# One sink matmul per pair of heads in a fused attention and MLP kernel, and steady steps whose parts are ordered by eight lists

## The chip, the core and the metric

The kernel runs on one core of a Trainium2 chip. A core has a matrix engine (PE, with PEld for its weight loads), a vector engine (DVE), an activation engine (ACT), a general engine (POOL), a queue engine (SP) that issues most DMAs here, and two on-chip memories: SBUF, and PSUM with eight banks into which PE writes. Each engine runs its own instructions in program order and waits on semaphores for the others. The metric is the device time of one launch in microseconds (us); three runs of the kernel before took 714.06, 714.3 and 715.22 us, median 714.3.

## What is computed

Windowed attention with sink tokens (4 batches, 8 heads, 768 positions, head size 64), then a two-layer MLP with softplus on the joined heads:

```python
scores = scale * np.matmul(q, k.transpose(0, 1, 3, 2))
is_sink = pos[None, :] < int(n_sink)                 # n_sink = 4
in_window = (rel >= 0) & (rel < int(window))         # window = 128
scores = np.where(is_sink | in_window, scores, -1e9)
a = softmax(scores)                                  # with + 1e-9 in the denominator
x = (a @ v).transpose(0, 2, 1, 3).reshape(B * S, H * D)   # 3072 x 512
h = x @ w_in                                         # 512 -> 2048
g = np.maximum(h, 0.0) + np.log1p(np.exp(-np.abs(h)))
out = g @ w_out                                      # 2048 -> 512
```

## The kernel before

The 3072 rows are worked through in 12 chunks of 256 rows (three to a batch). A chunk has eight attention steps, one per head, and the MLP of a chunk runs one chunk later, also in eight steps, one per block of 256 of the 2048 hidden columns. So a steady step is one head of chunk k beside one block of chunk k - 1. The first two chunks are computed in plain fp32 ("exact" in the code); from the third chunk on every fp32 operand is split into a high part (fp32r) and a low part, and products are made of high and low parts: three matmuls for the MLP (`up` L495, `down_part` L546 to L548), two for the scores (L260, L261).

What a steady step does for head h of its chunk, with the letter that the code has for it:

- `p` (`split`) and `q` (`split_v`): high and low parts of the next heads' q, k and v (`qkh`, `kl`, `vv`).
- `S` (`scores`): four matmuls into two tiles `s`, four heads ahead. `T` (`softmax`): DVE masks the scores and takes the row minimum into `a` and `stats` (L275, L281), ACT takes the exponentials with their row sums (L282). `N` (`normalise`): DVE adds 1e-9 and takes reciprocals (`sm` L288, `rc` L289), mostly POOL scales `a` (L296).
- `W` (`weights_t`): PE transposes the weights of head h into the PSUM tile `t`; ACT copies the high part `th`, DVE takes the low part `tl`; POOL selects the band from both into `pt` (L340, L343).
- `k` and `K` (`sink_weights`, `sink`), once per four heads: DVE scales the weights of the eight sink columns (`sa` L301), PE transposes them into `ts`, ACT and DVE write high and low parts into rows 0 to 31 and 32 to 63 of the constant tile `sk`.
- `V` (`values`): PE accumulates into the PSUM tile `x`: first the sink matmul (L362, `sk` against the sink values `vs` of this one head), then three matmuls of `pt` against `vv` (L369).
- `O` (`out`): `x` holds three partial sums (rows 0 to 63 of its first and second half, rows 64 to 127 of its first half). ACT copies one of them to SBUF (`xt`), DVE adds the other two (L387, L388) into `xf`, which joins two heads. After an odd head ACT and POOL (DVE for the last head) take high and low parts `xh` and `xl`, the MLP's input.
- `U` (`up`): 24 matmuls into `h`. `F` (`softplus`): three ACT passes. `P` (`gate`): DVE makes `mt` (L510) and the high part `gh`; `R` (`residue`): DVE makes the low part `gl` a step later. `D` and `E` (`down`): six matmuls each into the two tiles `acc`, two steps behind `U`; after a chunk's last block both are copied and stored.

All eight PSUM banks are taken: two by `acc`, two by `h`, two by `s`, one by `t` and `ts` together, one by `x`. So the tiles `t` and `ts` follow each other in one bank, and so do the tiles `x` of successive heads.

Nothing reorders the work afterwards: each engine's program is in the order in which the code issues it. A list of letters written out by hand (`START`) gives it for the first part, up to step 16. From step 17 on (the 18th) a loop issues the loads of a step and then the letters of one of two lists, one for the first head of a chunk, the other for all the rest:

```python
Ctx.STEADY = ("kWRqpUKFSTDPNVOE", "kqWRpSDKTUFNPVEO")
for i in range(2 * H + 1, (n + 1) * H + lag + 1):
    for part in "JjGL" + c.STEADY[i % H == 0]:
        run, ahead = parts[part]
        run(i + ahead)
```

A letter issues everything that belongs to it, on all engines, at one place. Behind the letters of three of eight steps come two DVE reductions that check a split weight (`room`, L476).

Of the kernel before, what the change touches and what calls it, by code (L numbers as in the profile page):

```python
# [127 lines left out]
class _Attention:  # L128
# [10 lines left out]
    def load_sinks(self):  # L139
        c, nc, b = self.c, self.c.nc, self.b  # L140
        raw = c.lp.tile([64, 2, D], F32, tag="vsr", name=f"vsr{b}", bufs=1)
        nc.sync.dma_start(raw[:], c.a["vs"][b].unsqueeze(0).broadcast_to([2, 32, 2, D]))
        c.vsr[b] = raw

    def sinks(self, g):
# [11 lines left out]
        vs = c.vst[g] = c.lp.tile([P, G, P], F32R, tag=f"vs{g}", name=f"vs{g}", bufs=1)  # L157
        _zero(nc, vs[64:].rearrange("p (a e) d -> p a (e d)", a=2), c.sk[64:].bitcast(F32).unsqueeze(1).broadcast_to([64, 2, CT]))
        for part in range(2):
            self.sinks_place(g, part)  # L160

    def sinks_high(self):
        c, nc, b = self.c, self.c.nc, self.b
        c.vsh[b] = c.lp.tile([64, 2, D], F32R, tag="vsh", name=f"vsh{b}", bufs=1)
        nc.gpsimd.tensor_scalar(c.vsh[b][:], c.vsr[b][:], 1.0, 0.0, ALU.mult, ALU.add)
# [98 lines left out]
    def softmax(self, h):  # L264
# [11 lines left out]
        for j in range(CH):  # L276
# [5 lines left out]
            nc.scalar.activation(a, a, AF.Exp, bias=nm, scale=-1.0, accum_out=sm[:, j : j + 1])  # L282
# [41 lines left out]
    def weights_t(self, h):
# [3 lines left out]
        for j in range(CH):  # L328
            nc.tensor.transpose(t[:, j], self.a[h // G][:, h % G, j, :P], c.ident[:])  # L329
# [3 lines left out]
        if not self.exact:
            tl = c.sp.tile([P, CH, P], F32, tag="tl", name=f"tl{chunk}_{h}", bufs=1)
            _sub(nc, "V", tl[:], t[:], th[:])
            parts.append(tl)
# [11 lines left out]
    def values(self, h):  # L348
# [12 lines left out]
        if not (self.exact and odd):
            nc.tensor.matmul(x[:, 0], sv, self.sk[h // G], start=True, stop=False, skip_group_check=True)  # L362
        v = self.v[h // 2]
        for n in range(self.vlo, 3):
# [4 lines left out]
            nc.tensor.matmul(x[:, :, o], w, pt[:, :, m], start=False, stop=last, skip_group_check=True)  # L369
        self.x[h] = x  # L370

    def out(self, h):
# [14 lines left out]
        nc.vector.tensor_tensor(tmp[:], x[:D, 0], tmp[:], ALU.add)  # L387
        nc.vector.tensor_tensor(self.xf[r0 : r0 + D], x[:D, 1], tmp[:], ALU.add)  # L388
# [601 lines left out]
```

## Time and profile before

| what | value |
|---|---|
| median of three runs | 714.3 us |
| the profiled execution | 714.26 us, span 712.5 us |
| weights arriving and being split beside the first chunks, with gaps on PE | to about 107 us |
| attention beside the MLP | to about 656 us |
| the last MLP steps, without attention | to 705.5 us |

The largest group of each of three engines:

```profile
L495 PE MATMUL h<-xh,wi 128*128 128x256 f32 x1536 | 253.5, 287 | 0.4 <-DVE mt L510 0.4
L56 DVE TENSOR_TENSOR gl<-mt,gh 128x512 fp32r<-128x512 f32 x96 | 79.1, 824 | 0.2
L296 POOL TENSOR_SCALAR a<-a,rc 128x128 f32<-128x128 f32 x178 | 67.4, 391 | 184.0 <-DVE rc L289 156.4
```

These are rows of the groups of instructions: line, engine, operation, output and input by the names in the program with their shapes, count; then busy us in all and mean ns of one; then the idle time of the engine just before them and what ended it. A matmul's 287 ns runs to its modelled end, and the next one starts long before that, so the sum of such times is no time on the clock. POOL's 184 us of idle time ahead of its scaling cost nothing, since POOL waits there for work that comes once in a step.

### The profile page before, as it was taken

Reading aid. Unit: us, or ns where it says so; the run is one execution under the profiler, and the core shown is the slowest. Engines: PE = TensorE matmul, PEld = TensorE weight load, DVE = VectorE, ACT = ScalarE, POOL = GpSimd, SP = SyncE. Lnnn points to the kernel's source line nnn. Section 1 sums busy time; section 2 is a strip of 40 time slices with the busy share of each in tenths; the row PEclk is TensorE's granted clock in tenths of the full one; section 3 lists DMA queues with packets and bytes.
Section 4 is the critical chain, followed back from the end, with each engine's and each line's share of the span. In section 5 each row is a group of like instructions: output and inputs, shape, how many; then the busy total and the mean of one; then the engine's idle time right before and its main releaser. Section 6 shows DMA issues by size and latency. Waiting matters only on the chain.

```text
span 712.5 us, 13842 instructions
## 1 busy us (share of the span) xinstructions
PE 695.6 (98%) x4536; PEld 627.4 (88%) x4536; DVE 578.3 (81%) x1657; ACT 452.9 (64%) x1113; POOL 369.5 (52%) x676
## 2 busy tenths in 40 slices
PE   8998899999999999999999999999999999999996
PEld 7887779899989989899998989999998989999995
DVE  7999999888888987887887887888888888865541
ACT  5879866657666666666666666666666765753431
POOL 6767457555554555565555655564554555542000
PEclk9999999999999999999999999999999999999999
DMA  9985523213122221311321321312222221100001
GB/s 321 372 325 207 168 71 100 63 59 94 46 80 80 69 67 61 102 46 47 111 59 50 109 69 51 108 49 65 81 71 69 80 75 55 61 12 1 30 2 34
DMA packets 39341, 64.52 MB, mean 91 GB/s; under 512 B 4508, under 2 KB 19932, under 8 KB 39260
## 3 DMA queue, kind: packets, MB, share of 16 engines
q1 hardware_dynamic: 38826, 63.02, 28.0%
q8 instruction: 38, 0.62, 0.4%
q10 hardware_dynamic: 434, 0.52, 0.2%
q14 instruction: 43, 0.35, 0.2%
HBM read 57.24 MB, written 6.29 MB: 89 GB/s over the span
## 4 chain that ended last, share of the span: by engine, by line
PE 90%; DVE 4%; ACT 3%; DMA 1%; issue 0%; POOL 0%; SPq 0%; ACTq 0%; POOLq 0%
PE h L495 37%; PE acc L546 12%; PE acc L547 12%; PE acc L548 12%; PE x L369 5%; PE s L260 3%; PE s L261 3%; PE t L329 3%; PE x L362 2%; DMA wo50r<-w 1%; ACT a L282 1%; PE word_ps L660 1%; PE ts L313 1%; ACT upper L48 1%; PE s L257 1%; DVE wt L439 1%
## 5 line engine op out<-in xcount | busy, mean ns | idle before, releaser
L495 PE MATMUL h<-xh,wi 128*128 128x256 f32 x1536 | 253.5, 287 | 0.4 <-DVE mt L510 0.4
L495 PEld LDWEIGHTS h<-xh,wi 128*128 128x128 f32 x1536 | 211.2, 191 | 1.7 <-DVE mt L510 0.6
L296 POOL TENSOR_SCALAR a<-a,rc 128x128 f32<-128x128 f32 x178 | 67.4, 391 | 184.0 <-DVE rc L289 156.4
L495 PE MATMUL h<-xl,wi 128*128 128x256 f32 x768 | 154.8, 283 | 1.6 <-DVE xl L56 1.6
L546 PE MATMUL acc<-wo,gh 128*128 128x512 f32 x384 | 152.3, 397 | 0.3 <-ACT gh L48 0.3
L548 PE MATMUL acc<-wo,gl 128*128 128x512 f32 x384 | 150.8, 393 | 0.3 <-DVE gl L56 0.3
L547 PE MATMUL acc<-wo,gh 128*128 128x512 f32 x384 | 151.0, 393 | 0.0
L495 PEld LDWEIGHTS h<-xl,wi 128*128 128x128 f32 x768 | 119.5, 192 | 2.0 <-DVE xl L56 2.0
L502 ACT ACTIVATE mt<-h 128x512 f32<-128x512 f32 x96 | 57.0, 594 | 98.7 <-PE h L495 98.7
L510 DVE SCALAR_TENSOR_TENSOR mt<-h,mt 128x512 f32<-128x512 f32 x96 | 66.1, 689 | 63.8 <-ACT mt L504 56.1
L282 ACT ACTIVATE a<-a,stats 128x136 f32<-128x136 f32 x192 | 76.1, 397 | 38.9 <-DVE stats L281 38.9
L548 PEld LDWEIGHTS acc<-wo,gl 128*128 128x128 f32 x384 | 72.1, 188 | 17.9 <-DVE gl L56 1.2
L546 PEld LDWEIGHTS acc<-wo,gh 128*128 128x128 f32 x384 | 72.1, 188 | 13.5 <-ACT gh L48 0.8
L547 PEld LDWEIGHTS acc<-wo,gh 128*128 128x128 f32 x384 | 72.3, 188 | 8.8
L56 DVE TENSOR_TENSOR gl<-mt,gh 128x512 fp32r<-128x512 f32 x96 | 79.1, 824 | 0.2
L340 POOL TENSOR_SCALAR_AFFINE_SELECT pt<-tl 128x256 fp32r<-128x256 f32 x80 | 59.1, 738 | 23.0 <-DVE tl L56 22.7
L340 POOL TENSOR_SCALAR_AFFINE_SELECT pt<-th 128x256 fp32r<-128x256 f32 (+1 forms) x96 | 46.4, 483 | 40.4 <-ACT th L48 38.8
L503 ACT ACTIVATE mt<-mt 128x512 f32<-128x512 f32 x96 | 60.8, 633 | 3.1
L504 ACT ACTIVATE mt<-mt 128x512 f32<-128x512 f32 x96 | 60.7, 633 | 3.0
L48 ACT CAST qkh<-qk 128x656 fp32r<-128x656 f32 x80 | 59.5, 744 | 0.4 <-DMA qk<-qk 0.4
L56 DVE TENSOR_TENSOR kl<-qk,qkh 128x400 fp32r<-128x400 f32 x80 | 51.5, 644 | 2.5
L56 DVE TENSOR_TENSOR tl<-t,th 128x256 f32<-128x256 f32 x80 | 33.2, 414 | 23.3 <-ACT th L48 23.3
(191 smaller groups left out, 1248.3 us busy)
## 6 DMA issues: line engine op xcount, KB each, us to landing
qk<-qk SPq DMA_DIRECT2D x160, 164.0 KB, 3.0
out<-o SPq DMA_DIRECT2D x23, 256.0 KB, 2.2
vr<-v SPq DMA_DIRECT2D x28, 192.0 KB, 2.5
q<-q SPq DMA_DIRECT2D x7, 256.0 KB, 5.6
k<-k SPq DMA_DIRECT2D x8, 200.0 KB, 8.1
vz<-v SPq DMA_DIRECT2D x4, 384.0 KB, 7.9
vr<-v SPq DMA_DIRECT2D x12, 128.0 KB, 2.1
vz<-v SPq DMA_DIRECT2D x4, 256.0 KB, 4.1
```

The costliest lines, as they stand in the source:

```text
L48: nc.scalar.copy(out, in_)
L56: (nc.vector if eng == "V" else nc.gpsimd).tensor_tensor(out, a, b, ALU.subtract)
L282: nc.scalar.activation(a, a, AF.Exp, bias=nm, scale=-1.0, accum_out=sm[:, j : j + 1])
L296: (nc.vector if eng == "V" else nc.gpsimd).tensor_scalar(a, a, rc[:, j : j + 1], 0.0, ALU.mult, ALU.add)
L340: nc.gpsimd.affine_select(pt[:, e, :, 1], src[:], [[0, CH], [1, P]], ALU.is_ge, 0.0, base=0, channel_multiplier=-1)
L495: nc.tensor.matmul(h[:, j], wt, x, start=k == 0, stop=k >= len(prods) - 2, skip_group_check=True)
L503: nc.scalar.activation(t[:], t[:], AF.Exp, scale=-1.0)
L504: nc.scalar.activation(t[:], t[:], AF.Ln, bias=1.0)
L510: nc.vector.scalar_tensor_tensor(t[:], h[:], 0.0, t[:], ALU.max, ALU.add)
L546: nc.tensor.matmul(acc[:], gh[:, j, q], wh, start=f == 0, stop=False, skip_group_check=True)
L547: nc.tensor.matmul(acc[:], gh[:, j, q], wl, start=False, stop=False, skip_group_check=True)
L548: nc.tensor.matmul(acc[:], gl[:, j, q], wh, start=False, stop=f == 2 * FP - 1, skip_group_check=True)
```

## The change

Four things are changed together.

1. The sinks. The sink values `vs` keep one column block of 64 per head, and `vs` and `sk` use all 128 rows: rows 0 to 63 of `sk` are high and low parts as before, rows 64 to 127 a copy of them by POOL; the high part of the sink values stands behind rows 0 to 63, the low part behind 64 to 127. One matmul against the columns of two heads then gives the sink sums of a pair. It is issued for even heads only, into a tile `xs` in the bank of `t`, and ACT copies it into `xf`.
2. The sum. `x` no longer starts with the sink matmul. DVE adds the three parts of `x` to `xf` one after the other, and ACT's copy `xt` goes.
3. Steps in one-engine parts. A letter issues its first part, and the rest is kept under a small letter and issued where that letter stands: `h` (`ql`, `kl`), `Q` (`vl`), `e` (exponentials), `n` (scaling), `t` (`th`), `u` (`tl`), `B` (selects), `X` and `x` (`xh`, `xl`), `g` (`gh`), `Y` (stores).
4. Eight lists, one for each step of a chunk, in place of two. The list up to step 16 is the same.

```diff
+    def do(self, kind, step):
+        if self.later is None:
+            step()
+        else:
+            self.later.setdefault(kind, []).append(step)
+    def now(self, kind):
+        for step in self.later.pop(kind, ()):
+            step()
...
         if not self.exact:
             _sub(nc, "V", sk[G * NS : 2 * G * NS], t[: G * NS], sk[: G * NS])
+            _copy(nc, "P", sk[2 * G * NS :], sk[: 2 * G * NS])
...
             x = c.ps_x.tile([P, 2, CT], F32, tag="x", name=f"x{chunk}_{h}")[:]
-            sv = c.vs[self.b, h // G][:, h % G]
-        if not (self.exact and odd):
-            nc.tensor.matmul(x[:, 0], sv, self.sk[h // G], start=True, stop=False, skip_group_check=True)
+            if not odd:
+                sv = c.vs[self.b, h // G][:, h % G : h % G + 2].rearrange("p h d -> p (h d)")
+                t = c.ps_t.tile([P, CT], F32, tag="t", name=f"xs{chunk}_{h}")
+                nc.tensor.matmul(t[:], sv, self.sk[h // G], start=True, stop=True)
+                self.xs(h, t)
...
-        tmp = c.sp.tile([D, CT], F32, tag="xt", name=f"xt{chunk}_{h}", bufs=1)
-        _copy(nc, "A", tmp[:], x[D:, 0])
-        nc.vector.tensor_tensor(tmp[:], x[:D, 0], tmp[:], ALU.add)
-        nc.vector.tensor_tensor(self.xf[r0 : r0 + D], x[:D, 1], tmp[:], ALU.add)
+        xf = self.xf[r0 : r0 + D]
+        for part in (x[:D, 0], x[:D, 1], x[D:, 0]):
+            nc.vector.tensor_tensor(xf, part, xf, ALU.add)
...
+    def xs(self, h, t):
+        self.xf = c.sp.tile([P, CT], F32, tag="xf", name=f"xf{chunk}_{h}")
+        _copy(nc, "A", self.xf[:], t[:])
...
-            for part in "JjGL" + c.STEADY[i % H == 0]:
-                run, ahead = parts[part]
-                run(i + ahead)
+            for part in "JjGL" + c.STEADY[i % H]:
+                if part in parts:
+                    run, ahead = parts[part]
+                    run(i + ahead)
+                else:
+                    c.now(part)
...
-Ctx.STEADY = ("kWRqpUKFSTDPNVOE", "kqWRpSDKTUFNPVEO")
+Ctx.STEADY = [
+    "kWtuDpQSqTBKyhenURXNVFPEYOgx",
+    "WqtkQyuUSpDhTFEPKnRBgxVeXNYO",
...
```

What this does on the engines, at three places of chunk 7. A name such as `x7_2_5762` is the tile `x` of chunk 7, head 2, with a running number. First PE, where the values of head 2 begin, behind the first six down matmuls; before:

```order
L546 MATMUL acc6_1_5748<-wo00_512,gh6_0_5558 128x512
L547 MATMUL acc6_1_5748<-wo00_512,gh6_0_5558 128x512
L548 MATMUL acc6_1_5748<-wo00_512,gl6_0_5593 128x512
L362 MATMUL x7_2_5762<-sk_66,vs0_1342 128x256
L369 MATMUL x7_2_5762<-pt7_2_5693,vv7_1_5595 128x2x128
L369 MATMUL x7_2_5762<-pt7_2_5693,vv7_1_5595 128x512
```

and after the change, at the same place:

```order
L604 MATMUL acc6_1_5730<-wo00_516,gh6_0_5562 128x512
L605 MATMUL acc6_1_5730<-wo00_516,gh6_0_5562 128x512
L606 MATMUL acc6_1_5730<-wo00_516,gl6_0_5637 128x512
L405 MATMUL xs7_2_5741<-sk_66,vs0_1346 128x256
L414 MATMUL x7_2_5740<-pt7_2_5713,vv7_1_5570 128x2x128
L414 MATMUL x7_2_5740<-pt7_2_5713,vv7_1_5570 128x512
```

The sink matmul has kept its place for this even head and writes `xs`; at head 3 no such row is left ahead of the values.

Second DVE, from the making of `mt` for block 2 of chunk 6 to the low part `tl` of the next head; before:

```order
L510 SCALAR_TENSOR_TENSOR mt6_2_5730<-h6_2_5705,mt6_2_5730 128x512
L50 CAST gh6_2_5756<-mt6_2_5730 128x512
L288 TENSOR_SCALAR sm7_6_5740<-sm7_6_5740 128x2
L289 RECIPROCAL rc7_1_5516<-sm7_6_5740 128x2
L387 TENSOR_TENSOR xt7_2_5768<-x7_2_5762,xt7_2_5768 64x256
L388 TENSOR_TENSOR xf7_2_5767<-x7_2_5762,xt7_2_5768 64x256
L476 TENSOR_REDUCE room_64<-wi41_858 128x1 x2
L56 TENSOR_TENSOR tl7_3_5788<-t7_3_5783,th7_3_5786 128x256
L56 TENSOR_TENSOR gl6_2_5795<-mt6_2_5730,gh6_2_5756 128x512
```

and after the change:

```order
L563 SCALAR_TENSOR_TENSOR mt6_2_5718<-h6_2_5675,mt6_2_5718 128x512
L307 TENSOR_SCALAR sm7_6_5722<-sm7_6_5722 128x2
L308 RECIPROCAL rc7_1_5487<-sm7_6_5722 128x2
L59 CAST gh6_2_5750<-mt6_2_5718 128x512
L430 TENSOR_TENSOR xf7_2_5743<-x7_2_5740,xf7_2_5743 64x256 x3
L529 TENSOR_REDUCE room_64<-wi41_862 128x1 x2
L65 TENSOR_TENSOR gl6_2_5798<-mt6_2_5718,gh6_2_5750 128x512
L65 TENSOR_TENSOR tl7_3_5805<-t7_3_5770,th7_3_5803 128x256
```

Two adds have become three, and `gl` now stands ahead of `tl`.

Third DVE at the change of chunks, from `mt` of the last block of chunk 5 to the low part that goes into `sk` for heads 0 to 3 of chunk 7; before:

```order
L510 SCALAR_TENSOR_TENSOR mt5_7_5426<-h5_7_5401,mt5_7_5426 128x512
L50 CAST gh5_7_5450<-mt5_7_5426 128x512
L288 TENSOR_SCALAR sm7_3_5436<-sm7_3_5436 128x2
L289 RECIPROCAL rc7_0_5146<-sm7_3_5436 128x2
L387 TENSOR_TENSOR xt6_7_5460<-x6_7_5456,xt6_7_5460 64x256
L388 TENSOR_TENSOR xf6_6_5363<-x6_7_5456,xt6_7_5460 64x256
L56 TENSOR_TENSOR xl6_4778<-xf6_6_5363,xh6_4777 128x256
L301 TENSOR_TENSOR sa7_0_5477<-a7_0_5145,rc7_0_5146 128x64
L56 TENSOR_TENSOR tl7_0_5484<-t7_0_5479,th7_0_5482 128x256
```

and after the change:

```order
L563 SCALAR_TENSOR_TENSOR mt5_7_5404<-h5_7_5373,mt5_7_5404 128x512
L430 TENSOR_TENSOR xf6_6_5344<-x6_7_5436,xf6_6_5344 64x256 x3
L59 CAST gh5_7_5443<-mt5_7_5404 128x512
L307 TENSOR_SCALAR sm7_3_5420<-sm7_3_5420 128x2
L308 RECIPROCAL rc7_0_5128<-sm7_3_5420 128x2
L65 TENSOR_TENSOR xl6_4767<-xf6_6_5344,xh6_4766 128x256
L325 TENSOR_TENSOR sa7_0_5463<-a7_0_5127,rc7_0_5128 128x64
L65 TENSOR_TENSOR tl7_0_5470<-t7_0_5465,th7_0_5468 128x256
```

The adds now stand directly behind `mt`, and `gh`, `sm` and `rc` between the adds and `xl`.

More of the change, by code (lines that the diff above doesn't have):

```diff
@@ L90, in _constants @@
     make_identity(nc, c.ident)
-    c.hmask = cp.tile([64, G], F32, name="hmask")
+    c.hmask = cp.tile([P, G], F32, name="hmask")
     nc.gpsimd.memset(c.hmask[:], 1.0)
-    for e in (0, 32):
+    for e in range(0, P, 32):
         m = c.hmask[e : e + 32]
@@ L156, in sinks, with sinks_place @@
             self.sinks_low()
[L157 to L160, printed above, removed]
+        c.vst[g] = c.lp.tile([P, G, D], F32R, tag=f"vs{g}", name=f"vs{g}", bufs=1)
+        self.sinks_place(g)
     def sinks_high(self):
         c, nc, b = self.c, self.c.nc, self.b
-        c.vsh[b] = c.lp.tile([64, 2, D], F32R, tag="vsh", name=f"vsh{b}", bufs=1)
+        c.vsh[b] = c.lp.tile([P, 2, D], F32R, tag="vsh", name=f"vsh{b}", bufs=1)
         nc.gpsimd.tensor_scalar(c.vsh[b][:], c.vsr[b][:], 1.0, 0.0, ALU.mult, ALU.add)
     def sinks_low(self):
-        raw = self.c.vsr[self.b]
-        self.c.nc.gpsimd.tensor_tensor(raw[:], raw[:], self.c.vsh[self.b][:], ALU.subtract)
-    def sinks_place(self, g, part):
+        c, b = self.c, self.b
+        low = c.vsh[b][D:]
+        c.nc.gpsimd.tensor_tensor(low, c.vsr[b][D:], low, ALU.subtract)
+    def sinks_place(self, g):
         c, b = self.c, self.b
         c.vs[b, g] = c.vst[g]
-        src = (c.vsh, c.vsr)[part][b]
-        self._place(c.vst[g][:64, :, part * D : part * D + D], src[:, g : g + 1], 64)
+        self._place(c.vst[g][:], c.vsh[b][:, g : g + 1], P)
     def _place(self, out, src, rows):
@@ L281, in softmax, with exps @@
             nc.vector.tensor_tensor_reduce(a, self.s.pop((h, j))[:, :KW], m[:], -SCALE, BIG, ALU.add, ALU.min, nm)
-            nc.scalar.activation(a, a, AF.Exp, bias=nm, scale=-1.0, accum_out=sm[:, j : j + 1])
+        c.do("e", lambda: self.exps(h))
+    def exps(self, h):
+        c, nc = self.c, self.c.nc
+        for j in range(CH):
+            a = self.a[h // G][:, h % G, j]
+            k = (self.chunk * H + h) * CH + j
+            sm = self.sm[h][:, j : j + 1]
+            nc.scalar.activation(a, a, AF.Exp, bias=c.stats[:, k : k + 1], scale=-1.0, accum_out=sm)
     def normalise(self, h):
@@ L332, in weights_t, with weights_low, select @@
         parts = [th]
[L333 to L336, printed above, removed]
+        if self.exact:
+            c.do("B", lambda: self.select(h, parts))
+        else:
+            c.do("u", lambda: self.weights_low(h, t, parts))
+    def weights_low(self, h, t, parts):
+        c, nc, chunk = self.c, self.c.nc, self.chunk
+        tl = c.sp.tile([P, CH, P], F32, tag="tl", name=f"tl{chunk}_{h}", bufs=1)
+        _sub(nc, "V", tl[:], t[:], parts[0][:])
+        parts.append(tl)
+        c.do("B", lambda: self.select(h, parts))
+    def select(self, h, parts):
+        c, nc, chunk = self.c, self.c.nc, self.chunk
+        th = parts[0]
         lo = 1 if self.first else 0
@@ L368, in values @@
             last = n == 2 and (odd or not self.exact)
-            nc.tensor.matmul(x[:, :, o], w, pt[:, :, m], start=False, stop=last, skip_group_check=True)
+            first = n == self.vlo and not self.exact
+            nc.tensor.matmul(x[:, :, o], w, pt[:, :, m], start=first, stop=last, skip_group_check=True)
         self.x[h] = x
@@ L530, in down @@
                 if j == 1:
-                    self.store(t)
+                    self.store(t, self.acc[t])
             return
@@ L647, in next_sinks @@
             return
-        if k < n and att[k].first and 0 < e < 6:
+        if k < n and att[k].first and 0 < e < 5:
             a = att[k]
-            if e < 4:
-                (a.load_sinks, a.sinks_high, a.sinks_low)[e - 1]()
-            else:
-                a.sinks_place(0, e - 4)
-        elif att[k - 1].first and k - 1 > c.EXACT and e < 2:
-            att[k - 1].sinks_place(1, e)
+            (a.load_sinks, a.sinks_high, a.sinks_low, lambda: a.sinks_place(0))[e - 1]()
+        elif att[k - 1].first and k - 1 > c.EXACT and e == 0:
+            att[k - 1].sinks_place(1)
     def fill(n):
@@ L900, in _kernel @@
                 _fast(c)
-            c.last = False
+            c.last, c.later = False, None
         ok = nc.values_load(c.flag[:1, :1], min_val=0, max_val=1)
```

53 lines of the change are left out of this document (41 added, 12 removed).

## The prediction

> **What bounds the kernel now.** I read the page first: busy shares, the slices, the chain that ended last.
>
> ```profile
> span 712.5 us, 13842 instructions
> PE 695.6 (98%) x4536; PEld 627.4 (88%) x4536; DVE 578.3 (81%) x1657; ACT 452.9 (64%) x1113; POOL 369.5 (52%) x676
> PE   8998899999999999999999999999999999999996
> DVE  7999999888888987887887887888888888865541
> PEclk9999999999999999999999999999999999999999
> PE 90%; DVE 4%; ACT 3%; DMA 1%; issue 0%; POOL 0%; SPq 0%; ACTq 0%; POOLq 0%
> ```
>
> PE carries 90% of the chain, and its granted clock never falls, so the clock explains nothing here. A busy PE may still hide waits, so next come the busy times by stretch, PE's waits, and the chain in order of time inside the steady part.
>
> ```profile
> 50.00:100.00 50.00, 45.44 (x281) 39.04 (x280) 48.64 (x122) 42.69 (x97) 29.16 (x40) 1.00 0.54 173
> 158.38:325.32 166.94, 166.94 (x1110) 151.75 (x1110) 141.41 (x413) 110.09 (x273) 92.74 (x171) 1.00 0.24 72
> PEld ts L313 <- DVE tl L56: 0.7, 3, 0.2
> ...
> 246.44 2.88 PE h L495 x24
> ...
> 251.20 0.12 PE x L362
> 251.32 0.47 PE x L369 x3
> ...
> 253.18 0.22 PE t L329 x2
> ```
>
> The columns of the stretches are length, then PE, PEld, DVE, ACT and POOL busy. Before about 107 us PE has gaps. From there to 700 us it has none: the three chunks from 158.38 to 325.32 are full to the last digit, and the only wait recorded for PE between 107 and 700 us is that of the weight load of `ts`, 0.7 us in three cases. One step (one head, one block of the MLP) is 253.18 - 246.22 = 6.96 us of back-to-back matmuls. So in this stage a matmul taken off PE is worth its slot on the chain, as long as what feeds PE still comes in time. DVE is the next engine: 141.41 of 166.94 us, 85%.
>
> **The sink matmuls.** 80 of them (10 chunks of 8 heads) become 40.
>
> ```profile
> L362 PE MATMUL x<-sk,vs x80: 279/279/283, 105.1 to 652.9; 128*128 128x256 f32 x80
> ```
>
> The 279 ns is one matmul from start to modelled end; the next begins long before. What counts is its slot on the chain, 0.12 us above (251.20 to 251.32). 40 x 0.12 = **4.8 us** less. They run from 105.1 to 652.9 us, all but the first inside the full stretch, so nothing else hides them. Were each worth its whole 279 ns, the gain would be 11.2 us; the full stretch excludes that, since the spacing is seen.
>
> The Trainium skill ("TensorE: Matmul & The Clock Gate", Back-to-back issue gap) gives N/2.4 + 2.5 ns, 109 ns for N = 256, against 120 ns in the trace; by it the gain would be an estimated 4.4 us. The measured slot decides.
>
> **The adds.** Each head had one ACT copy (64x256) and two DVE adds; now it has three DVE adds, and each pair one ACT copy of 128x256.
>
> ```profile
> L48 ACT COPY xt<-x 64x256 f32<-64x256 f32 x80 | 29.7, 372 | 2.0
> L48 ACT CAST th<-t 128x256 fp32r<-128x256 f32 x79 | 29.6, 374 | 25.0 <-PE t L329 23.0 <-issue 1.1
> 232.04 0.40 DVE L387 TENSOR_TENSOR xt<-x,xt 64x256 f32<-64x256 f32 x1
> 232.47 0.42 DVE L388 TENSOR_TENSOR xf<-x,xt 64x256 f32<-64x256 f32 x1
> 232.81 1.26 DVE L476 TENSOR_REDUCE room<-wi 128x1 f32<-128x512 f32 x2
> ...
> 238.96 0.42 DVE L388 TENSOR_TENSOR xf<-x,xt 64x256 f32<-64x256 f32 x1
> 239.41 0.23 DVE L301 TENSOR_TENSOR sa<-a,rc 128x64 f32<-128x64 f32 x1
> ```
>
> ACT: 80 x 0.372 goes, 40 x 0.374 (the nearest copy of that shape) comes: 14.8 us less, off the path. DVE: a dependent add takes 0.43 us from start to start (232.04 to 232.47), so 80 x 0.43 = 34 us more. That costs nothing as long as it fits into DVE's idle time beside PE's matmuls. Over the three chunks DVE would be busy 141.4 + 24 x 0.43 = 151.7 us. PE then needs 166.94 - 12 x 0.12 = 165.5 us. DVE may thus idle 13.8 us, where it idled 25.5. Nearly half of its waits must go, or DVE becomes the bound. That is the main risk, and the lists decide it.
>
> After an add into the upper rows (odd heads) the next instruction starts 0.45 us on, after one into the lower rows 0.34 us on (the two pairs of rows above). The Trainium skill ("VectorE: DVE Perf Modes", Two Vector instructions with no wait between them) has a rule for this: an instruction whose input or output starts in another quadrant than the last one is held until all earlier ones end. The trace agrees. By that rule the third add, which reads `x` from row 64, holds its follower also in even heads: an estimated 0.1 us more for 40 heads, 4 us of DVE in all, 1.2 us of the 13.8. It speaks against the change but takes no sign from it.
>
> **The order.** Most lists keep PE's order (transposes, up, scores, down, values, down). What is moved is when DVE, ACT and POOL do their parts. On SP the order is unchanged, and the loads still open each step, so no transfer is moved. I look at three places.
>
> First `ts` in the step of head 0, the tightest of before:
>
> ```profile
> 265.20 0.69 DVE L510 SCALAR_TENSOR_TENSOR mt<-h,mt 128x512 f32<-128x512 f32 x1 [0.54 <-ACT mt L504]
> 266.97 0.42 DVE L388 TENSOR_TENSOR xf<-x,xt 64x256 f32<-64x256 f32 x1
> 267.86 0.43 DVE L56 TENSOR_TENSOR xl<-xf,xh 128x256 fp32r<-128x256 f32 x1 [0.47 <-ACT xh L48]
> 268.34 0.42 DVE L56 TENSOR_TENSOR tl<-t,th 128x256 f32<-128x256 f32 x1
> 267.42 0.41 ACT L48 CAST xh<-xf 128x256 fp32r<-128x256 f32 x1 [1.08 <-DVE xf L388]
> 268.98 0.38 PE L313 MATMUL ts<-ident,sa 128*32 128x128 f32 x2
> ```
>
> The bank of `t` is free at 268.34 + 0.42 = 268.76 us, and `ts` starts at 268.98. After the change the adds come right behind `mt`: 265.20 + 0.72, then 0.43 + 0.43 + 0.42 gives xf at 267.20; `xh` ends at 267.63. `gh`, `sm` and `rc` fill that wait (0.34 + 0.28), `xl` starts near 267.74, 0.12 earlier, and `tl` ends near 268.64. PE arrives 0.12 us earlier too, having one sink matmul less. The margin stays as it was: some 0.2 us, no stall but no room. The third add is paid by `mt`'s wait of 0.54 us and by the idle time at `xl`.
>
> Second, the bank of `t` now also takes the sink sums `xs` of even heads; the next head's transposes wait for ACT's copy of it.
>
> ```profile
> 249.36 0.60 ACT L502 ACTIVATE mt<-h 128x512 f32<-128x512 f32 x1 [1.40 <-PE h L495]
> 252.09 0.37 ACT L48 COPY xt<-x 64x256 f32<-64x256 f32 x1
> ```
>
> The up matmuls end at 249.32, and ACT is through softplus and exponentials at 252.09, 2.77 us on; the copy ends 3.14 us on. PE reaches the transposes at 253.18, 3.86 us on, so 0.7 us is to spare. In head 6 `xh` stands ahead of the copy (0.41 us): 0.3 us. In head 4 `sk` stands ahead of softplus, but `ts` delays PE as well: about 0.5 us. In head 0 the copy stands ahead of softplus and has over a microsecond.
>
> Third, `sk` gets a POOL copy (64x256) ahead of the sink matmul, 20 times.
>
> ```profile
> L165 POOL TENSOR_SCALAR vsh<-vsr 64x128 fp32r<-64x128 f32 x4 | 1.3, 318 | 5.4 <-DMA vsr<-vs 5.4
> L60 POOL TENSOR_SCALAR sk<-room 128x256 fp32r<-128x256 f32 x1 | 0.4, 397 | 0.0
> PE h L495 <- DVE xl L56: 1.6, 2, 1.1
> PE x L369 <- POOL pt L343: 0.4, 1, 0.4
> ```
>
> No row shows that copy; between 0.32 and 0.40 us I take 0.40, same free size. From head 0 on, up (2.88 us) lies between `ts` and `xs`, and from head 4 on, scores and down (1.9 us); ACT's and DVE's parts of `sk` plus 0.40 are about 1.7 us. It is hidden, by least in head 4.
>
> Chunk 2's first head still runs in the hand-ordered start. There `xs` follows `sk` closely and may wait 0.1 us (at most 0.4). The larger `hmask` adds four selects of about 0.19 us on POOL near the beginning, ahead of a wait of 2.0 us for the sink values' DMA, which covers them. POOL makes the sink weights with fewer operations, which could end PE's 0.4 us wait for `pt`; the 1.1 us wait for `xl` hangs on DVE. Bounds for the start: -0.4 to +1.2 us. I take +0.1.
>
> **Sum.** The profiled execution took 714.26 us, its span 712.5; the median of the three shown is 714.3, the same. 714.26 - 4.8 + 0.1 + 0.4 = 709.96, **710.0 us**. The 0.4 is my allowance for small stalls at the tight places: two more hand-overs of 0.23 us (0.7/3, the wait at `ts`).
>
> **Rivals.**
> Late hand-overs eat the gain. A chunk has four `xs` and two `ts`, 60 in all. If a third come late by 0.23 us, 20 x 0.23 = 4.6 us go: 714.1. For it: margins of 0.2 to 0.3 us. Against: a stall gives DVE and ACT time to catch up.
>
> DVE becomes the bound, and it gets slower. Price per three chunks:
>
> ```profile
> DVE mt L510 <- ACT mt L504: 10.1, 16, 1.4
> DVE tl L56 <- ACT th L48: 7.0, 9, 0.9
> DVE sm L288 <- ACT a L282: 2.2, 3, 0.7
> ```
>
> If only the 7.0 us at `tl` go and the other 18.5 of the 25.5 us stay, three chunks take 151.7 + 18.5 = 170.2 us, 3.3 more than now, and ten take 11 more: **725 us**. The point from which this decides: over 15.2 us of idle time left (166.94 - 151.7) is slower than before. For it: 0.43 us a head on an engine 85% busy, and the steps with two reductions (1.19 us from 232.81 to the next) fill DVE wholly. Against: the lists move `tl` behind `gl` or `sa` and the adds ahead of `gh`, so those waits are filled, as worked out at `ts`; odd steps have about 1 us to give back.
>
> The matmul's slot is not worth its time, PE being held by something that the records hide: 714.3 us. The unbroken chain speaks against it.
>
> **Chances.** Forecast 0.66 (709.1 to 712.8, up to 0.3 us of stalls a chunk), late hand-overs 0.14, DVE bound 0.17, hidden slot 0.03. A measurement of this kernel tells about 0.2% (1.4 us) from no change. Faster is the forecast, 0.66; same the second and the fourth, 0.17; slower 0.17. The range leaves out the DVE case and little else: from 708.9 (a little below 714.26 - 4.8 - 0.4 = 709.06) to 715.5 (the late hand-overs with the start's +1.2).
>
> **What would show it.** Right: the three-chunk stretch PE-full and about 1.4 us shorter, DVE near 92% busy, `tl`'s and `mt`'s waits below 14 us together. Wrong: waits of PE's weight loads at `t` on ACT's `xs` copy or at `ts` on DVE's `tl` (late hand-overs), or PE below 99% between 160 and 600 us behind `x`, `s` or `acc` with DVE as releaser (DVE bound). If PE is full and the steps are no shorter, the slot of the sink matmul was hidden.

## The result, and the profile after

The changed kernel is **slower** by 0.6%, clear of the noise: median 718.79 us (four runs, 718.53 to 719.29) against 714.23 us (four runs of before), ratio 1.0061, 95% interval 1.0046 to 1.0077. The forecast was 710.0 us. The page of the kernel after, its profiled execution 718.53 us, by the same rows as before:

```profile
span 716.7 us, 13788 instructions
...
PE 694.9 (97%) x4496; PEld 622.5 (87%) x4496; DVE 607.7 (85%) x1737; ACT 429.7 (60%) x1073; POOL 356.5 (50%) x690
...
PE   8998999999999999999999999999999999999996
...
DVE  7999989898998988988998998988998899876442
...
PE 71%; DVE 16%; ACT 3%; issue 2%; POOL 0%; DVEq 0%; POOLq 0%; ACTq 0%
```

PE still looks full in tenths, but its share of the chain fell from 90% to 71% and DVE's rose from 4% to 16%. The groups of after show the exchange itself:

```profile
L430 DVE TENSOR_TENSOR xf<-x,xf 64x256 f32<-64x256 f32 x240 | 100.6, 419 | 6.7
L405 PE MATMUL xs<-sk,vs 128*128 128x256 f32 x40 | 12.4, 310 | 0.7 <-POOL sk L61 0.7
L61 POOL TENSOR_SCALAR sk<-sk 64x256 fp32r<-64x256 f32 x20 | 9.2, 459 | 7.0 <-DVE sk L65 5.8 <-DVE s L286 0.6
```

40 sink matmuls, 240 adds, 20 copies of `sk`, as the diff says. Next the stretch of three chunks, from one `ts` of head 0 to the third after it, 166.94 us before (columns as there: length, then PE, PEld, DVE, ACT and POOL busy):

```profile
158.54:327.13 168.59, 166.82 (x1096) 150.51 (x1096) 150.25 (x437) 103.03 (x261) 88.88 (x176) 1.00 0.24 71
```

It is 1.65 us longer, not 1.4 shorter, and PE is no longer busy to its end. Which waits these are, from the waits of after between 110 and 655 us (before had there 0.7 us at `ts`, in three cases):

```profile
PEld ts L337 <- DVE tl L65: 7.3, 12, 1.0
PE ts L337 <- DVE tl L65: 4.7, 9, 0.7
PEld xs L405 <- POOL sk L61: 3.7, 10, 0.6
```

Nine waits of PE for `tl`, one in each chunk, at the one place that the prediction called the tightest: `ts` in the step of head 0. (The three more of the weight load are at `ts` of head 4.) The recorded idle time is not all of it, since a matmul's busy time runs to its modelled end: the last matmul of `s` in the rows below starts at 270.19, so `ts` could have followed 0.12 us later, at 270.31. It starts at 271.00, 0.69 us late where 0.53 are recorded. With 0.16 us more for each of nine, the 4.7 us are about 6.1. First PE, then DVE in the timeline of after, ahead of that `ts`:

```profile
270.19 0.28 PE L272 MATMUL s<-kl,qkh 128*128 128x264 f32 x1
271.00 0.39 PE L337 MATMUL ts<-ident,sa 128*32 128x128 f32 x2 [0.53 <-DVE tl L65]
```

```profile
257.98 0.55 DVE L286 COPY_PREDICATED s<-diag,s 128x128 f32<-128x128 int32 x2 [0.63 <-PE s L272]
...
259.93 0.68 DVE L563 SCALAR_TENSOR_TENSOR mt<-h,mt 128x512 f32<-128x512 f32 x1
...
260.99 0.70 DVE L307 TENSOR_SCALAR sm<-sm 128x2 f32<-128x2 f32 x1
261.73 0.17 DVE L308 RECIPROCAL rc<-sm 128x2 f32<-128x2 f32 x1
261.81 1.32 DVE L430 TENSOR_TENSOR xf<-x,xf 64x256 f32<-64x256 f32 x3
263.06 1.26 DVE L529 TENSOR_REDUCE room<-wo 128x1 f32<-128x512 f32 x2
264.35 0.42 DVE L65 TENSOR_TENSOR tl<-t,th 128x256 f32<-128x256 f32 x1
...
267.25 0.68 DVE L563 SCALAR_TENSOR_TENSOR mt<-h,mt 128x512 f32<-128x512 f32 x1
267.96 1.33 DVE L430 TENSOR_TENSOR xf<-x,xf 64x256 f32<-64x256 f32 x3
269.32 0.43 DVE L59 CAST gh<-mt 128x512 fp32r<-128x512 f32 x1
...
270.52 0.42 DVE L65 TENSOR_TENSOR tl<-t,th 128x256 f32<-128x256 f32 x1
```

DVE's last recorded wait is the first row here, 0.63 us for PE at `s` in the step of head 6; from there to the end of `tl`, 13 us on, it has none. `mt` carried a wait of 0.54 us for ACT in before; here ACT's last pass over `mt` ends at 265.95 + 0.63 = 266.58, and DVE comes to it only at 267.25:

```profile
265.95 0.63 ACT L557 ACTIVATE mt<-mt 128x512 f32<-128x512 f32 x1
```

### The profile page after: what moved, and what is told of

The parts are those of the page before. It is cut to its first block, busy times and chain, and to the rows that moved or that the text cites. A ratio compares the mean times of both kernels' runs of the same rounds, so it can differ in the third digit from the quotient of the medians.

```text
span 716.7 us, 13788 instructions
## 1 busy us (share of the span) xinstructions
PE 694.9 (97%) x4496; PEld 622.5 (87%) x4496; DVE 607.7 (85%) x1737; ACT 429.7 (60%) x1073; POOL 356.5 (50%) x690
## 4 chain that ended last, share of the span: by engine, by line
PE 71%; DVE 16%; ACT 3%; issue 2%; POOL 0%; DVEq 0%; POOLq 0%; ACTq 0%
PE h L548 31%; PE acc L604 9%; PE acc L605 9%; PE acc L606 9%; PE x L414 4%; DVE xf L430 3%; PE t L354 2%; PE s L271 2%; PE s L272 2%; DVE room L529 2%; DVE mt L563 1%; DVE tl L65 1%; DVE kl L65 1%; DVE gl L65 1%; DVE gh L59 1%
## 5 line engine op out<-in xcount | busy, mean ns | idle before, releaser
L430 DVE TENSOR_TENSOR xf<-x,xf 64x256 f32<-64x256 f32 x240 | 100.6, 419 | 6.7
L320 POOL TENSOR_SCALAR a<-a,rc 128x128 f32<-128x128 f32 x178 | 78.5, 452 | 39.6 <-DVE rc L308 38.2
L380 POOL TENSOR_SCALAR_AFFINE_SELECT pt<-tl 128x256 fp32r<-128x256 f32 x80 | 48.9, 611 | 78.6 <-DVE tl L65 78.6
L380 POOL TENSOR_SCALAR_AFFINE_SELECT pt<-th 128x256 fp32r<-128x256 f32 (+1 forms) x96 | 41.8, 436 | 70.9 <-ACT th L57 70.5
L65 DVE TENSOR_TENSOR gl<-mt,gh 128x512 fp32r<-128x512 f32 x96 | 69.5, 724 | 0.5
L65 POOL TENSOR_TENSOR vv<-vr,vv 128x384 fp32r<-128x384 f32 (+1 forms) x40 | 41.3, 1032 | 36.8 <-ACT vv L57 36.7
```

Source lines behind the costliest of these rows:

```text
L65: (nc.vector if eng == "V" else nc.gpsimd).tensor_tensor(out, a, b, ALU.subtract)
L320: (nc.vector if eng == "V" else nc.gpsimd).tensor_scalar(a, a, rc[:, j : j + 1], 0.0, ALU.mult, ALU.add)
L380: nc.gpsimd.affine_select(pt[:, e, :, 1], src[:], [[0, CH], [1, P]], ALU.is_ge, 0.0, base=0, channel_multiplier=-1)
L430: nc.vector.tensor_tensor(xf, part, xf, ALU.add)
```

## The experiments

Theory A: DVE has time enough over a chunk, but is late at one place, at `tl` ahead of `ts` of head 0. Theory B: with the third add DVE is full everywhere, and every repair only moves the wait. Theory C: the lists do the harm, the sinks alone would gain. All kernels below are edits of the changed kernel. Kernels of one group shared their runs of before (medians 714.44, 714.41, 714.63 and 714.45 us).

| run | median us | ratio to before, 95% interval |
|---|---|---|
| e1_old_lists | 736.03 | 1.0289 to 1.0323 |
| e2_old_sinks | 713.98 | 0.9986 to 1.0005 |
| e3_ts_early | 713.85 | 0.9985 to 1.0004 |
| e4_two_adds | 708.24 | 0.9895 to 0.9929 |
| e5_checks_early | 727.18 | 1.0162 to 1.0190 |
| e6_xl_early | 717.74 | 1.0031 to 1.0058 |
| e7_all | 718.97 | 1.0047 to 1.0074 |
| e8_lists_only | 712.62 | 0.9963 to 0.9983 |
| e9_checks_gap | 716.75 | 1.0019 to 1.0042 |
| e10_sk_early | 711.67 | 0.9946 to 0.9973 |
| e11_both | 711.64 | 0.9949 to 0.9976 |
| e12_no_pool_copy | 715.65 | 1.0011 to 1.0030 |

A profile is that of one execution; those of e9 (714.90 us) and e12 (714.73 us) are among the shorter ones of their kernels.

### The parts of the change

New sinks and sum under the two lists of before, nothing kept for small letters:

```diff
-        c.later = {}
-Ctx.STEADY = ["kWtuDpQSqTBKyhenURXNVFPEYOgx", ...
+Ctx.STEADY = ["kqWRpSDKTUFNPVEO"] + 7 * ["kWRqpUKFSTDPNVOE"]
```

> New sinks and new sum, but the two lists of before, each step's letter issuing all its parts at once. Theory A (DVE has time over the chunk as a whole, but with the new lists it comes late at one place, tl ahead of ts in the step of head 0): the lists are not the cause as such, and without them DVE keeps the waits of before beside 0.43 us more a head, so this is slower than the change, 722 to 745 us. Theory B (DVE is full everywhere through the third add): the same direction, 745 us if the 25.5 us of idle time per three chunks stay. Theory C (the new lists do the harm, the sinks alone gain): 709 to 711 us.

736.03 us. Theory C has fallen: without the lists the sinks and the sum cost 21.6 us (736.03 - 714.44). The waits of this run between 110 and 655 us show three places where PE is now held:

```profile
PE ts L337 <- DVE tl L65: 7.2, 9, 0.9
PE t L354 <- ACT xf L57: 6.5, 9, 0.8
PE xs L405 <- POOL sk L61: 4.8, 6, 1.0
```

They are the three places of the prediction. The lists clear the second, and only lessen the first and the third.

The opposite, the eight lists with the sinks and the sum of before:

```diff
-        xf = self.xf[r0 : r0 + D]
-        for part in (x[:D, 0], x[:D, 1], x[D:, 0]):
-            nc.vector.tensor_tensor(xf, part, xf, ALU.add)
+        _copy(nc, "A", tmp[:], x[D:, 0])
+        nc.vector.tensor_tensor(tmp[:], x[:D, 0], tmp[:], ALU.add)
+        nc.vector.tensor_tensor(self.xf[r0 : r0 + D], x[:D, 1], tmp[:], ALU.add)
...
```

> The eight lists and the one-engine parts, but sinks and sum as before (80 sink matmuls into x, ACT copy and two adds). A and B: without the third add DVE comes in time, PE is full with the old number of matmuls: 713.5 to 715 us, no wait of 0.5 us or more at ts. C: the waits at ts of head 0 stay at 0.5 to 0.9 us a chunk, and it takes 718 to 721 us.

713.98 us, no change. The lists alone neither gain nor lose.

The new sinks and lists with two adds a head, so that one of the three parts is left out of the sum:

```diff
-        for part in (x[:D, 0], x[:D, 1], x[D:, 0]):
+        for part in (x[:D, 0], x[:D, 1]):
```

> The change without the third add (the part of x in rows 64 to 127 is left out of the sum). A and B: 0.43 us a head less on DVE ends the wait at ts: 709 to 711 us. C (lists, not adds): the waits at ts stay, 717 to 719 us.

708.24 us, below what was expected. Its stretch of three chunks:

```profile
157.38:322.87 165.49, 165.49 (x1099) 150.84 (x1097) 139.95 (x412) 102.67 (x261) 87.50 (x176) 1.00 0.25 73
```

PE is full again, and the stretch is 165.49 us, where the prediction had 165.5 (166.94 less 12 slots of 0.12). So a sink matmul was worth its slot, and the whole loss hangs on the third add: 168.59 - 165.49 = 3.10 us per three chunks, and 718.53 - 708.22 = 10.3 us between the two profiled executions. DVE's busy time differs by 150.25 - 139.95 = 10.3 us for 24 adds, 0.43 each, as priced.

### Is DVE full, or late at one place?

`tl` and `sa` go ahead of `gh` and `xl` at the `ts` of head 0; no work is added or removed:

```diff
-    "kWtuDpQSqTBKyhenURXNVFPEYOgx",
+    "WtukXxgDpQSqTBKyhenURNVFPEYOgx",
...
-    "qWtkQUuRpFSDTBeKhyPVOXgNEnYx",
+    "qWtkQUuRpFSDTBeKhyPVONEnY",
```

> The change, with the two lists at the change of chunks edited: tl and sa ahead of xl and gh on DVE, th ahead of xh on ACT, for the step of head 0. A: tl is done some 0.6 us earlier, so about 0.6 us a chunk comes back, nine chunks: 5.5 us, 713 us. B: the wait moves to xl or another place, and at most 1 us comes back: 717.5 to 719 us. C: as A.

713.85 us, 4.9 us less for the same DVE work, where B allowed 1 us at most. A holds, though the time is only that of before.

Next the cause of the lateness. The two reductions of head 6's step go to the end of head 0's:

```diff
-            if i >= 2 * H + lag and i % H in (2, 4, 6) and checks:
+            if i >= 2 * H + lag and i % H in (0, 2, 4) and checks:
```

> The changed kernel, but the two weight reductions that stood at the end of the step of head 6 (1.26 us of DVE, 205.18 to 206.44 in the run with tl early) stand at the end of the step of head 0, behind the ts that waits. DVE has exactly as much to do as before. A (DVE has time over the chunk and is late at one place): the steps ahead of ts get 1.26 us of room, more than the longest wait there (0.90), so the nine waits of ts for tl (4.7 us in the list of waits, 6.2 us from matmul to matmul) go but for a few tenths: 712 to 713.5 us. It could lose 0.5 where the reductions now delay the step of head 1. B (DVE full over the whole chunk): the wait moves elsewhere, 717.5 to 719.

727.18 us: both theories missed, and the place is what they missed. From the timeline of this run, DVE in the steps of heads 0 to 2, then PE at the values of head 2:

```profile
221.43 0.69 DVE L563 SCALAR_TENSOR_TENSOR mt<-h,mt 128x512 f32<-128x512 f32 x1 [2.36 <-ACT mt L557]
...
223.75 1.26 DVE L529 TENSOR_REDUCE room<-wo 128x1 f32<-128x512 f32 x2
225.04 0.42 DVE L65 TENSOR_TENSOR tl<-t,th 128x256 f32<-128x256 f32 x1
...
231.95 0.42 DVE L65 TENSOR_TENSOR tl<-t,th 128x256 f32<-128x256 f32 x1
```

```profile
233.85 0.73 PE L414 MATMUL x<-pt,vv 128*128 128x256 f32 x3 [0.97 <-POOL pt L383]
```

DVE stands idle for 2.36 us ahead of `mt`, and the reductions come behind it. From there DVE has no wait for 11 us, `tl` of head 2 is late, so are POOL's selects `pt`, and PE stands 0.97 us at the values of head 2. An engine can be idle for 2 us and late 10 us on. The `ts` of head 0 did gain: by the starts of the matmuls it is 0.32 to 0.44 us late in this run, and 0.47 to 0.90 in the changed kernel.

So the same reductions, put into that gap:

```diff
-    "kWtuDpQSqTBKyhenURXNVFPEYOgx",
+    "kWtuDpQSqTBKyhenURXNVFCPEYOgx",      (C: the two reductions of this step)
-            ... i % H in (2, 4, 6) and checks:
+            ... i % H in (2, 4) and checks:
```

> The changed kernel, but the two reductions of the step of head 6 stand in the step of head 0 ahead of mt, where DVE waits 1.8 to 2.4 us for ACT in every chunk (in the run with the reductions moved behind mt, that wait stayed 1.97 us and the reductions came on top, which made tl and pt of heads 1 and 2 late). DVE does the same work. A (DVE has time over the chunk, and what counts is where its work stands): the nine waits of ts for tl go but for a tenth or two each, and no new wait comes: 711.5 to 713.5 us. B (DVE full over the chunk): 717.5 to 719 as before, or worse as with the other place (727).

716.75 us, 10 us better than in the other place with the same work, but only 2.0 better than the changed kernel, and short of what A expected. The timeline of this run shows why:

```profile
263.69 0.54 DVE L286 COPY_PREDICATED s<-diag,s 128x128 f32<-128x128 int32 x2 [0.73 <-PE s L272]
...
265.64 0.69 DVE L563 SCALAR_TENSOR_TENSOR mt<-h,mt 128x512 f32<-128x512 f32 x1
...
268.91 0.42 DVE L65 TENSOR_TENSOR tl<-t,th 128x256 f32<-128x256 f32 x1
```

```profile
264.74 0.63 ACT L557 ACTIVATE mt<-mt 128x512 f32<-128x512 f32 x1
```

ACT (second fence) is through at 265.37, and DVE comes to `mt` at 265.64, 0.27 us late. The list of head 7 has `T` (masks of `s`) ahead of `h` (the split). With 1.26 us given back DVE just waits 0.73 us for PE at `s`, with the split queued behind, and `mt` stays late, by less. So the reductions were one cause of the lateness, and the order of `T` and `h` looks like a second behind it: in all nine chunks of this run `mt` comes 0.24 to 0.27 us late, however long DVE waits at `s` (0.60 to 0.98 us). No run changes that order alone.

The third cause tried: POOL's `xl`, early in the list of head 6, so that it doesn't run beside `sm`.

```diff
-    "WqkRtuUQBySpTFhPenDXgKVENOYx",
+    "WqkRtuXUQBxySpTFhPenDgKVENOY",
```

> The changed kernel, but in the list of head 6 the pair's xh (ACT) and xl (POOL) come ahead of the exponentials and of the row sums, so that POOL's xl no longer runs beside DVE's sm (0.70 us there, 0.16 in the other steps). If sm is long because POOL's subtraction runs beside it, DVE gains 0.5 us ahead of each ts of head 0: the waits fall from 0.47/0.69/0.90 to about 0/0.2/0.4 us, 714.5 to 716 us. If sm is long by its place on DVE, or the time is lost on another DVE instruction that now meets xl, nothing changes: 718 to 719. Theory B (DVE full everywhere) expects at most the 0.5 x 10 = 5 us of DVE time as well, and so cannot be told from A here; this run prices one of the causes.

717.74 us. `sm` is short again, and POOL's `xl` has ended before it (timeline of this run, DVE, then POOL):

```profile
261.50 0.17 DVE L307 TENSOR_SCALAR sm<-sm 128x2 f32<-128x2 f32 x1
```

```profile
258.68 0.74 POOL L65 TENSOR_TENSOR xl<-xf,xh 128x256 fp32r<-128x256 f32 x1
```

And PE's waits at `ts`, 4.7 us in the changed kernel, in the list of waits of this run:

```profile
PE ts L337 <- DVE tl L65: 2.8, 9, 0.4
```

So the cause of the 0.70 us is settled: POOL's `xl` beside `sm`. `sm` is 0.53 us shorter, 4.8 us for nine, of which 1.9 us came through on these waits and 1.1 us on the median, between the two expectations. The traces show where the rest stays: `mt` of head 7's step is still 0.33 to 0.40 us late here, where it was 0.36 to 0.73. The 0.24 to 0.27 us of the run before are still in that, and in one chunk of three DVE now waits 0.34 us for PE at `s`.

### A version that beats both

All repairs together, with the reductions at the end of head 0's step. New are `tl` ahead of `gl` in the lists of heads 2 and 4, and `R7` behind `V16` in the first list, so that DVE's `gl` leaves POOL's first copy of `sk` alone:

```diff
-    "WkRQtUqyupKShBFTeDnPVNgOYXxE",          (head 2)
+    "WkQtUquRypKShBFTeDnPVNgOYXxE",
-    "WQqkUtRupBhKSnTFDePygNVOYXEx",          (head 4)
+    "WQqkUtuRpBhKSnTFDePygNVOYXEx",
-... U8 P7 K16 R7 D6 N20 V16 p21 ...
+... U8 P7 K16 D6 N20 V16 R7 p21 ...
(heads 0, 6 and 7, and the place of the reductions: as above)
```

> All repairs together: tl and sa ahead of gh and xl at the ts of head 0, reductions out of the step of head 6, xl early in head 6, tl ahead of gl in the steps of head 2 and head 4, and in the start gl of block 7 behind the sink copy of POOL, whose 0.82 us beside gl delays the first steady sink matmul by 0.66 us. A: PE has no waits left between 110 and 655 us but some 0.1 us at xs, so the whole 4.8 us of the sink matmuls and 0.5 of the start remain: 709 to 710.5 us, faster than both kernels. B: DVE is at 91% in every step and each repair only moves the wait: 713 to 715.

718.97 us, above what either theory expected. The same lists with the reductions where the changed kernel has them:

```diff
-            if i >= 2 * H + lag and i % H in (0, 2, 4) and checks:
+            if i >= 2 * H + lag and i % H in (2, 4, 6) and checks:
```

> As the run with all repairs, but the reductions stay in the step of head 6. A: tl and sa come 0.35 us late in one of three chunks when only the order at ts is repaired; with xl early as well DVE gains 0.5 us there, so this wait goes too and the time is that of all repairs within 1 us, 709.5 to 711. If the reductions are what matters, 712 to 713.5. B: 713 to 715.

712.62 us, 6.4 us less, so the misplaced reductions ate the repairs in the run before. It is faster than the kernel before, 1.6 us above what A expected at most. It lies where it was expected if the reductions matter (712 to 713.5), but two runs on, moving them out of head 6's step gives nothing. What is left stands at `xs` of head 4. DVE, then POOL, in the timeline of this run, in chunk 4:

```profile
242.54 0.41 DVE L65 TENSOR_TENSOR sk<-ts,sk 32x256 fp32r<-32x256 f32 x1
242.88 0.47 DVE L286 COPY_PREDICATED s<-diag,s 128x128 f32<-128x128 int32 x2
```

```profile
243.41 0.40 POOL L61 TENSOR_SCALAR sk<-sk 64x256 fp32r<-64x256 f32 x1 [1.32 <-DVE s L286]
```

POOL begins 0.46 us after DVE's part of `sk` has ended (242.95). The run that follows was built on this row, but chunk 4 is an exception: in the nine other chunks POOL begins 0.17 us after DVE's part, as here in chunk 3 (DVE, then POOL):

```profile
187.23 0.41 DVE L65 TENSOR_TENSOR sk<-ts,sk 32x256 fp32r<-32x256 f32 x1
```

```profile
187.81 0.40 POOL L61 TENSOR_SCALAR sk<-sk 64x256 fp32r<-64x256 f32 x1 [1.06 <-DVE sk L65]
```

`xs` is late there too, by 0.18 to 0.22 us. What comes late is DVE's part, 0.51 us after ACT's has ended (186.72). So DVE's part is made earlier, `gl` (`R`) behind it and the split (`h`) ahead:

```diff
-    "WQqkUtuRpBhKSnTFDePygNVOYXEx",
+    "WQqkUtupBhKRSnTFDePygNVOYXEx",
```

> The run with the lists repaired (712.6), but in the step of head 4 DVE does head 9's split ahead of the second part of sk, and gl behind it. There sk's second part ended at 242.95, POOL's copy of sk began only at 243.41, when DVE's copies of s were over, and the sink matmul waited 0.2 to 0.47 us and its followers 0.1, in every chunk. If POOL was held by those copies of s, it now begins right behind sk's second part, near 242.6, and the waits of xs go: 3 us less, 709 to 710.5 us. If POOL's copy is lengthened by gl beside it (0.82 us, as in the start) half of that: 710.5 to 711.5. If the third part of sk has nothing to do with the wait: 712.6 as before.

711.67 us, ratio 0.996: **faster than both kernels**, by 3.0 us (714.63) and 7.1 us (718.79). Against the run before it is 0.95 us less, but the two intervals overlap, so this last step's gain isn't shown. The three-chunk stretch, then DVE and POOL at `sk` in chunk 3:

```profile
156.83:322.96 166.13, 166.11 (x1098) 150.60 (x1096) 149.07 (x437) 104.08 (x261) 90.48 (x176) 1.00 0.25 72
```

```profile
185.83 0.41 DVE L65 TENSOR_TENSOR sk<-ts,sk 32x256 fp32r<-32x256 f32 x1 [0.15 <-ACT sk L57]
186.28 0.69 DVE L65 TENSOR_TENSOR gl<-mt,gh 128x512 fp32r<-128x512 f32 x1
```

```profile
186.41 0.82 POOL L61 TENSOR_SCALAR sk<-sk 64x256 fp32r<-64x256 f32 x1 [0.58 <-DVE sk L65]
```

The stretch is 0.81 us shorter than before, of the 1.45 that two adds reach. DVE's part now stands directly behind ACT's, and POOL begins 0.17 us after it as before. But POOL's copy runs beside `gl` and takes 0.82 us in place of 0.40, so that `xs` is still 0.15 to 0.19 us late in nine of the ten chunks. That is the second case of the expectation (`gl` lengthens the copy, 710.5 to 711.5), 0.2 us above its range. In chunk 4 POOL again begins 0.45 us after DVE's part (241.50 to 241.95), now without the copies of `s`, so those are not the cause of that one delay. What it is stays open.

This and the reductions ahead of `mt` in head 0's step:

> The last two together: lists repaired, sk's copy early, and the reductions of head 6 ahead of mt in the step of head 0. A: with ts no longer waiting in the repaired lists the moved reductions have nothing left to give on PE but a few tenths: the same as the run with sk early, within 1 us, 708.5 to 710.5. Should DVE be late anywhere else in the steps of heads 6 and 7 it would be faster by more. B: 713 or more.

711.64 us, the same: in the repaired lists no wait of `ts` is left that the reductions could shorten. The time given back goes into DVE's wait for PE at `s` of head 7's step, 1.1 to 1.5 us in every chunk, where it was 0.34 in one of three and none in the others.

Last, `sk` without POOL for heads 4 to 7:

```diff
+            if g:
+                _copy(nc, "A", sk[2 * G * NS : 3 * G * NS], t[: G * NS])
+                _sub(nc, "V", sk[3 * G * NS :], t[: G * NS], sk[: G * NS])
+            else:
+                _copy(nc, "P", sk[2 * G * NS :], sk[: 2 * G * NS])
```

> The run with lists, sk and reductions repaired (711.6), but for the heads 4 to 7 of a chunk the third part of sk is no POOL copy: ACT writes the high part a second time from ts, and DVE subtracts a second time behind the first. With POOL, sk was whole 0.99 us after DVE's second part (242.48 against 241.50) and xs started 0.15 us late, its followers 0.1. If POOL's late start and slow pace beside DVE are what holds xs, sk is now whole 0.35 to 0.45 us after the second part, and the last steady waits of xs go (0.15 to 0.19 and 0.1 in each of ten chunks): 2.5 us less. Against it DVE has 0.34 us and ACT 0.27 us more per chunk ahead of mt; if DVE has room there: 709 to 710 us. If DVE is full from there to the next ts (B), the gain is lost again: 711 to 713.

715.65 us, worse by 4 us and above both expectations. In the timeline of this run, DVE, ACT and PE:

```profile
243.01 0.42 DVE L65 TENSOR_TENSOR sk<-ts,sk 32x256 fp32r<-32x256 f32 x1 [0.42 <-ACT sk L57]
```

```profile
242.62 0.36 ACT L57 CAST sk<-ts 32x256 fp32r<-32x256 f32 x1 [0.48 <-DVE sk L65]
...
245.62 0.35 ACT L57 COPY xf<-xs 128x256 f32<-128x256 f32 x1
```

```profile
246.02 0.44 PE L358 MATMUL t<-ident,a 128*128 128x128 f32 x2 [0.24 <-ACT xf L57]
```

The edit did not do what was meant: ACT's second copy waited 0.48 us for DVE's first part, and DVE's second subtraction 0.42 us for ACT's second copy, so the four ran one behind the other and `sk` came hardly earlier: `xs` is 0.10 to 0.14 us late in place of 0.15 to 0.19. And ACT, held up ahead of softplus, is late with `xf`, for which the transposes of head 5 now wait; they start 0.39 to 0.51 us late in each of nine chunks. The run doesn't tell what POOL's part costs.

## Why the prediction was wrong, step by step

**The slot.** Right: 12 slots of 0.12 us are 1.44 us, and the stretch with two adds is 1.45 us shorter and PE-full. The hidden slot is excluded.

**The adds' size.** Right: 0.43 us each, DVE busy 150.25 us per three chunks where 151.7 were forecast. The estimate of 0.1 us more in even heads by the Trainium skill ("VectorE: DVE Perf Modes", Two Vector instructions with no wait between them) was too much. The reductions start 1.25 us after the three adds of head 6 (261.81 to 263.06), `gh` 1.36 us after those of head 7 (267.96 to 269.32). That is 0.35 us for the last add of an even head and 0.46 for that of an odd one. The page keeps the last start in SBUF and that in PSUM apart, and the reductions read only SBUF; the prediction had read over that, and the trace agrees with the page.

**The first place, `ts` of head 0: the step that failed.** The prediction put the adds "right behind `mt`" and set `mt` at 265.20, where ACT lets it start, so that the third add was "paid by `mt`'s wait of 0.54 us and by the idle time at `xl`". That wait was gone. DVE came to `mt` 0.67 us after ACT (267.25 against 266.58), a swing of 1.2 us. The prediction's working of this place began at `mt` and took over when DVE gets there from the kernel before. In the changed kernel DVE is 0.27 us late already at `mt` of head 6's step (259.93, where ACT ends at 259.66), and from there it needs 7.32 us to the next `mt`, while ACT's ends are 6.92 us apart. Three things ahead of it were not followed:
- the third add of the step of head 6 too, which ends in two reductions and had no idle time to pay with (three adds 1.25 us, 261.81 to 263.06; two took 0.77 in before, 232.04 to 232.81);
- POOL's `xl` beside `sm` in that step (0.70 us in place of 0.16; shown by the run with `xl` early);
- `T` ahead of `h` in the lists of heads 6 and 7, by which DVE waits at `s` while ready work stands behind: 0.63 us in head 6's step (257.98), and 0.73 us in head 7's when the reductions are away. This one is argued from the traces; no run changes that order.

From `mt` to the end of `tl` it took 267.25 to 270.94, 3.69 us where 3.44 were worked out: 0.25 more, against a margin of 0.2. With 0.67 + 0.25 - 0.2 the 0.69 us of wait is explained, to a few hundredths. In the run with the reductions in the gap the same sum gives 0.27 + 0.25 - 0.2 = 0.32 us, and `ts` starts 0.32 us late there (269.39). The first term is the larger, and was forecast as zero.

**The second place, the bank of `t`.** Right: between 110 and 655 us no wait at `t` in the changed kernel. In the last run one more copy on ACT ahead of softplus brings it at once, in head 5, behind the `xs` of head 4, where 0.5 us had been worked out as spare.

**The third place, `sk`.** Least in head 4, as said, but not hidden. In the list of waits it is 3.7 us on the weight loads of `xs` in ten chunks. By the starts of the matmuls less is lost: `xs` is 0.03 to 0.07 us late in eight of them (0.34 in chunk 4, 0.24 in the last), and the matmul behind it 0.1 in each, some 2 us together. The price of 0.40 us for the copy was right (188.63 to 189.03). What was missing is DVE's lateness once more: it begins its part 0.33 us after ACT's has ended (187.72 to 188.05), with two adds 0.03 us, and with two adds `xs` is on time, to 0.02 us, in all chunks but the last. In the hand-ordered start it is more than the 0.4 us given as most: `xs` begins 0.66 us late there, with two adds as well. All waits of the changed kernel:

```profile
PEld xs L405 <- POOL sk L61: 4.6, 11, 0.9
```

4.6 us in all are 0.9 more than in the window from 110 us, and they belong to chunk 2's first head.

**The allowance.** 0.4 us were set aside for stalls; the third add brought 10.3 us. By the starts of the matmuls 6.7 of them are at `ts` (6.2 at head 0, 0.5 at head 4), some 1.5 at `xs` and behind it, and 1.1 at one place, the values of head 2 of chunk 2 (119.30), which wait for POOL's `pt`. About 1 us was not traced.

**The rivals.** The late hand-overs had the right place and signs (the weight load of `ts` waiting for `tl`), but a price of 0.23 us in a third of the cases, taken from the waits of before; it was 0.48 to 0.90 in every chunk, at one `ts` of two. The DVE rival had the right test: over 15.2 us of idle time left in three chunks is slower. 168.59 - 150.25 = 18.3 us were left, above the 16.7 us that DVE's measured busy time allows (166.94 - 150.25). Its mechanism, a full DVE, was wrong, since other orders of the same work take 7 us less. What bound the kernel was between the two: an engine with 11% of idle time, at the wrong places. So one sign of being right came true without the gain: the waits at `tl` and `mt` are 8.2 us in three chunks, below 14, but what counts is where they lie.

## What to carry to other kernels

Work put on an engine that is 85% busy is not paid by its idle time as such, but by the waits that lie between the last point where it was on time and the next point where another engine waits for it; follow the engine over that whole stretch, back to the last recorded wait, and not from the instruction whose wait you mean to use. When an order is written out by hand, put what is ready ahead of what waits: here one order of the same instructions took 727 us and another 712. A gap in one step doesn't help a wait that stands ahead of it in the same program.

## What was not expected of the hardware

`sm` is a DVE instruction on 128x2 numbers and takes 0.16 us. Started at 260.99, while POOL ran `xl`, it took 0.70 us:

```profile
260.82 0.85 POOL L65 TENSOR_TENSOR xl<-xf,xh 128x256 fp32r<-128x256 f32 x1 [2.64 <-ACT xh L57]
```

It ended at 261.69, 0.02 us after POOL's instruction (261.67), and so it is in nine chunks alike (0.70 to 0.71 us, ending 0.02 to 0.03 after POOL): it was held to POOL's end, whatever its own size. The Trainium skill ("SBUF — State Buffer", SBUF: two separate sides) has a rule for this: the port pair that DVE and POOL share is locked for a whole instruction by the one that starts first, and the other "fully blocks"; on DVE's side it holds for instructions in a two-port mode or with two inputs in SBUF. In which mode `sm` ran no trace shows, but the trace agrees, and the run with `xl` early (0.17 us) bears it out. The other way round, POOL's copy of `sk` started 0.13 us after DVE's `gl` in the version with `sk` early (186.41 against 186.28) and took 0.82 us in place of 0.40, to 0.26 us after the end of `gl` (187.23 against 186.97).
